# Attention times values on TensorE's two halves, in a kernel of windowed attention and a gated spatial mixer

## The chip, the cores and the metric

The kernel runs on one core of a Trainium2 chip. A core has five engines that run side by side and meet through semaphores: TensorE (PE, matrix products into PSUM), VectorE (DVE), ScalarE (ACT), GpSimd (POOL) and SyncE (SP), which here issues all DMAs. PSUM has eight banks of 512 float32 words for each of 128 partitions. The metric is the device time in microseconds (us) from one launch, inputs and output in HBM; lower is better.

## What is computed

One transformer layer for 2048 tokens of width 448, in bfloat16: normalisation, attention of 16 heads of 28 over 8 keys at distances 0, 2, ..., 14 back, a residual; then normalisation and a gated mixer whose gate is a 2048 x 2048 product over tokens.

```python
qkv = (x @ wqkv).reshape(B, S, 3, H, Dh)            # H=16, Dh=28, x normalised
idx = pos[:, None] - 2 * arange(8)[None, :]         # keys of a query; mask idx >= 0
logits = einsum('bhsd,bhswd->bhsw', q, kg) * Dh ** -0.5
attn = softmax(where(mask, logits, -1e9))
o = einsum('bhsw,bhswd->bhsd', attn, vg)            # attention times values
h = x + o.reshape(B, S, D) @ wo

z = gelu(layernorm(h) @ w_in)                       # 2 x 896 columns
z1, z2 = z[..., :896], layernorm(z[..., 896:])
g = einsum('ts,bsf->btf', w_sp, z2) + b_sp[None, :, None]
out = h + (z1 * g) @ w_out
```

## The kernel before

The attention works on 18 blocks of queries (112 to 128 tokens, GEOM, L17), each with 128 keys. The logits of a block are computed dense, keys by queries, head by head (L763, keys on the partitions); ACT takes exp of them into E (L772), and DVE multiplies E by a band mask that leaves the eight distances (L778, called mk below). Values carry a 29th column of ones (V1), so that one product gives both the weighted sum and the softmax's denominator: for each of 16 heads a matmul with E as the 128 x 128 stationary operand and 29 moving columns of V1 (L783 to L791, jobs o0 to o17). All 16 go into one PSUM bank, 32 words for a head. DVE takes the reciprocal of the 29th column (L795) and multiplies the other 28 by it (L798) into otm. A DMA transpose brings otm into OT (oT0 to oT17), for the later blocks by way of OTs and a copy (oc), and the projection with wo follows for pairs of 128 tokens (project, L720: y0, y2, ...), then the residual sum, the second normalisation and its transposes hT into hnT.

Most other products contract 448 = 7 x 64 rows, so they run in halves of the array: product (L486) pairs a matmul on rows 0 to 63 with one on rows 64 to 127, for two outputs in two banks. Its job A has four pairs and its job B three; in B the two halves of the array change banks, so that B waits for A's last matmul (`pl.apart`, own). Some other PE job must stand between A and B; the planner asserts it. Such products are qk (queries and keys), v, y, z1 and z2 (the two halves of the mixer's input). The logits use quarters of the array (28 rows). Full-array work is that of the values, the first transposes xT0 to xT3 (L647), the spatial product (L908) and the output product (L932). The code calls the three modes F (full), H (half) and L (quarter); SWITCH (L20) holds the planner's own costs for going from one to another.

Nothing is ordered at run time: every piece is a job with an engine; ORDER lists the jobs' numbers, and each engine runs its jobs in that sequence. BANK gives each product's first PSUM bank, ON says for some copies whether ACT, DVE or POOL makes them. Number 912 in ORDER is a filler matmul that keeps PE busy at the start. SP runs DMAs in its own sequence: tokens, weights, the transposes xT4 to xT15 of the normalised tokens, the oT and hT transposes, w_in, and 32 transposing loads of the spatial weights (wsp_la, wsp_lb, wsp_hi). Before a query/key product of 512 tokens can start, its four xT must have landed.

Of the kernel before, what the change touches and what calls it, by code (L numbers as in the profile page):

```python
# [6 lines left out]
D = 448  # L7
NHEAD = 16
DH = 28
# [16 lines left out]
ORDER = [21, 36, 112, 24, 22, 25, 0, 37, 38, 1, 44, 45, 35, 39, 40, 46, 47, 2, 116, 3, 121, 23, 912, 912, 912, 912, 912, 912,  # L26
# [82 lines left out]
ALU = mybir.AluOpType  # L109
# [213 lines left out]
def bass_sequential_preLN__sliding_local_dilated__mixer_gmlp__prompt_kernel(  # L323
# [12 lines left out]
    pl = Planner()  # L336
# [4 lines left out]
    with contextlib.ExitStack() as top:  # L341
# [404 lines left out]
        for b in range(NAB):  # L746
# [33 lines left out]
            tk = Ticket(1)  # L780
            vs = b % NV

            def fo(e, nq=nq, slot=slot, vs=vs, tk=tk):  # L783
                for g in range(4):
                    for hh in range(4):
                        h, ei = 4 * g + hh, 4 * hh + g
# [221 lines left out]
```

## Time and profile before

| | us |
|---|---|
| three runs | 240.85, 243.95, 241.71 (median 241.71) |
| the profiled execution | 240.89 |
| its span, first to last instruction | 239.2 |

The span is what the profile's rows lie in; 1.7 us of the execution lie around it. In the profile, a group's row gives line, engine, operation, output and inputs, shapes and count, then busy us, mean ns of one, and the engine's idle time just before, with what ended it. A row of the timeline gives start, length from the first start to the last end, engine, line and count; a bracket at its end is the idle time before it. The matmuls overlap one another, so their mean duration is longer than the interval at which they start.

### The profile page before, as it was taken

The numbers are of one execution on the slowest core, as the hardware profiler recorded it, in microseconds if no ns is written. First come the engines' busy times: TensorE is split into PE (matmuls) and PEld (weight loads), VectorE is DVE, ScalarE is ACT, GpSimd is POOL, SyncE is SP. The second block draws the span as 40 slices with busy tenths as digits, with TensorE's granted clock in tenths as the row PEclk, the third lists the DMA queues.
The fourth block names the chain that finished last, engine by engine and source line by source line (L and its number), as shares of the span: only waits on it lengthen the run. The fifth ranks groups of instructions, "written<-read, shape, count | busy, mean of one in ns | idle before, by whom it ended". The sixth has DMA issues, their size and how long they took to land.

```text
span 239.2 us, 4969 instructions
## 1 busy us (share of the span) xinstructions
PE 231.4 (97%) x2099; PEld 114.3 (48%) x2110; DVE 152.3 (64%) x323; ACT 92.0 (38%) x113; POOL 35.2 (15%) x73
## 2 busy tenths in 40 slices
PE   7989999799999999999999999999999999999995
PEld 2564464354555644444444444444444444444453
DVE  5799799979989987959877124410751222613674
ACT  3787988768789656687820000000000000000000
POOL 5154220440302030313124000000000000000000
DMA  6943538526668967979999970000000010000032
GB/s 202 340 119 69 137 70 142 89 60 124 148 106 165 171 108 157 154 149 165 168 192 166 186 189 0 3 0 0 0 0 3 31 47 0 0 3 0 26 108 97
DMA packets 66310, 23.26 MB, mean 97 GB/s; under 512 B 58608, under 2 KB 66160, under 8 KB 66288
## 3 DMA queue, kind: packets, MB, share of 16 engines
q1 hardware_dynamic: 66288, 22.95, 47.1%
q8 instruction: 16, 0.26, 0.4%
q14 instruction: 6, 0.05, 0.1%
HBM read 6.83 MB, written 1.84 MB: 36 GB/s over the span
## 4 chain that ended last, share of the span: by engine, by line
PE 81%; DVE 9%; DMA 4%; ACT 2%; SPq 2%; issue 1%; POOL 0%
PE psum L908 40%; PE psum L495 27%; PE psum L932 9%; DMA x_tm<-in_A_x_dram 3%; PE psum L763 2%; PE psum L787 2%; DVE st L607 2%; DVE E L778 2%; DMA xhT<-xn 2%; ACT E L772 1%; DVE z2p L505 1%; DVE otm L798 1%; SPq L520 1%; SPq L519 1%; DVE xn L618 1%
## 5 line engine op out<-in xcount | busy, mean ns | idle before, releaser
L908 PE MATMUL psum<-wsp_hi,z2p 128*128 128x512 bf16 x218 | 50.6, 379 | 0.3
L917 DVE TENSOR_TENSOR ub<-psum,bb 128x512 bf16<-128x512 f32 x28 | 19.2, 689 | 44.4 <-PE psum L908 43.9
L772 ACT ACTIVATE E<-psum 128x896 bf16<-128x896 f32 (+2 forms) x36 | 32.0, 934 | 9.0 <-PE psum L763 9.0
L908 PEld LDWEIGHTS psum<-wsp_hi,z2p 128*128 128x128 bf16 x224 | 21.9, 98 | 26.1
L495 PE MATMUL psum<-xhT,wqk 64*128 64x512 bf16 (+1 forms) x280 | 27.1, 334 | 2.0 <-DMA xhT<-xn 1.6
L908 PE MATMUL psum<-wsp_lb,z2p 128*128 128x512 bf16 x108 | 26.1, 379 | 0.2
L908 PE MATMUL psum<-wsp_la,z2p 128*128 128x512 bf16 x111 | 25.9, 379 | 0.2 <-issue 0.2
L495 PE MATMUL psum<-w_in,hnT 64*128 64x448 bf16 x224 | 24.8, 349 | 0.1
L495 PE MATMUL psum<-hnT,w_in 64*128 64x512 bf16 x196 | 24.1, 376 | 0.0
L939 DVE TENSOR_TENSOR srg<-psum,x_tm 128x448 bf16<-128x448 f32 (+1 forms) x17 | 9.7, 592 | 20.8 <-PE psum L932 20.7
L932 PE MATMUL psum<-w_out,z1p 128*128 128x448 bf16 (+1 forms) x119 | 22.3, 341 | 0.0
L843 DVE BATCH_NORM_STATS2 st<-z2p 128x6 f32<-128x448 bf16 x32 | 18.9, 609 | 3.7 <-ACT z2p L836 3.4
L778 DVE TENSOR_TENSOR E<-E,maskb 128x1792 bf16<-128x1792 bf16 (+2 forms) x18 | 19.6, 1095 | 1.7 <-ACT E L772 1.6
L607 DVE BATCH_NORM_STATS2 st<-x_tm 128x6 f32<-128x448 bf16 x32 | 19.4, 612 | 1.6 <-DMA x_tm<-in_A_x_dram 1.4
L602 POOL TENSOR_TENSOR rs<-rs,negh 128x2 f32<-128x2 f32 (+2 forms) x22 | 18.9, 857 | 1.8
L495 PEld LDWEIGHTS psum<-xhT,wqk 64*128 64x128 bf16 x280 | 12.8, 94 | 12.3 <-ACT E L772 2.4
L908 PEld LDWEIGHTS psum<-wsp_la,z2p 128*128 128x128 bf16 x112 | 10.9, 98 | 13.4 <-DVE z2p L852 0.4
L908 PEld LDWEIGHTS psum<-wsp_lb,z2p 128*128 128x128 bf16 x112 | 11.0, 98 | 13.2
L932 PEld LDWEIGHTS psum<-w_out,z1p 128*128 128x128 bf16 x119 | 11.6, 98 | 10.2 <-DVE z1p L920 0.3
L880 ACT ACTIVATE z1p<-psum 128x1024 bf16<-128x1024 f32 x14 | 14.2, 1023 | 5.2 <-PE psum L495 5.1
L495 PEld LDWEIGHTS psum<-w_in,hnT 64*128 64x128 bf16 x224 | 10.6, 94 | 11.0 <-DVE z2p L505 0.6
L601 POOL TENSOR_SCALAR rs<-mv 128x2 f32<-128x2 f32 (+2 forms) x22 | 6.3, 288 | 62.1 <-DVE mv L609 41.3
(54 smaller groups left out, 226.2 us busy)
## 6 DMA issues: line engine op xcount, KB each, us to landing
w_in<-in_B_w_in_dram SPq DMA_DIRECT2D x8, 224.0 KB, 3.0
out_dram<-srg SPq DMA_DIRECT2D x16, 112.0 KB, 1.7
x_tm<-in_A_x_dram SPq DMA_DIRECT2D x3, 448.0 KB, 6.1
wraw<-in_A_wqkv_dram SPq DMA_DIRECT2D x2, 448.0 KB, 4.1
w_out<-in_B_w_out_dram SPq DMA_DIRECT2D x1, 784.0 KB, 6.4
bb<-in_B_b_sp_dram SPq DMA_DIRECT2D x1, 512.0 KB, 5.8
wv<-in_A_wqkv_dram SPq DMA_DIRECT2D x2, 224.0 KB, 6.3
wo<-in_A_wo_dram SPq DMA_DIRECT2D x1, 336.0 KB, 7.7
```

Of the source, the lines that this page charges most:

```text
L495: ins = e.matmul(out(k), w(k, p0, c), x(k, p0, c), start=(k, p0, c) in first, stop=(k, p0, c) in last, tile_position=(p0, 0))
L601: [(lambda e: e.tensor_single_scalar(A, mv[:, m:m + n, 1], EPS, ALU.add), r_mv[k][m:m + n], [rr]), (lambda e: e.tensor_tensor(R, A, negh[: ...
L602: (lambda e: e.tensor_tensor(R, A, negh[:, 0:1].to_broadcast([128, n]), ALU.pow), [rr, r_negh], r_rs[k][m:m + n])],
L607: [(lambda e: e.bn_stats(st[:, m, :], src), [rsrc], [r_st[k][m]])], dve_t(D))
L772: return e.activation(o, i, AF.Exp, scale=SCALE)
L778: return e.tensor_tensor(a, a, maskb[:, 0:1, pad:pad + nq].to_broadcast([NK, NHEAD, nq]), ALU.mult)
L843: [(lambda e, m=m, k=k: e.bn_stats(st3[:, m, k, :], z2p[:, m, D * k:D * (k + 1)]), [r_z2[m]], [r_st[2][m]])], dve_t(D))
L880: return e.activation(o, i, AF.Gelu_apprx_tanh)
L908: ins = e.matmul(psv(tk), z2p[:, s, 128 * fc:128 * fc + 128], w[:, 512 * (tc % 2):512 * (tc % 2) + 512], start=(s == 0), stop=(s == NB - 1))
L917: [(lambda e, tc=tc, s=s, tk=tk: e.tensor_tensor(ub[:, s, :], psv(tk), bb[:, 512 * tc:512 * tc + 512], ALU.add), [r_bb], [r_ub[s]])], dve_ ...
L932: ins = e.matmul(psv(tk, 0, c1 - c0), z1p[:, fc, 128 * m:128 * m + 128], w_out[:, fc, c0:c1], start=(fc == 0), stop=(fc == FC7 - 1))
L939: [(lambda e, m=m, s=s, tk=tk, c0=c0, c1=c1: e.tensor_tensor(srg[:, s, c0:c1], psv(tk, 0, c1 - c0), x_tm[:, m, c0:c1], ALU.add), [r_x[m]], ...
```

## The change

The 16 matmuls of a block, each with all 128 keys, become 32, each with 64 keys: rows 0 to 63 of the array for the first half of the keys, rows 64 to 127 for the second. The block has two banks now, with eight heads in each. In job A the lower half of the array works on the eight heads of the first bank and the upper half on those of the second; in job B they change banks, so each head's sum is completed in PSUM by the second of its matmuls. Only the first matmul in each bank clears it (start), and the last closes it (stop). B waits for A as in product. DVE's two readers address two banks; they read as many elements as before.

With 18 jobs more, ORDER, BANK and ON are new as a whole: the order of all engines' work changes, and some copies change engine. Of the large casts, DVE has qe1_1, qe1_2, qe4_3, ve6 and four z2 casts before, and qe1_1, qe3_0, qe3_1 and two z2 casts after. The filler stands 16 times instead of 13.

```diff
-ORDER = [21, 36, 112, 24, 22, 25, 0, 37, 38, 1, 44, 45, 35, 39, 40, 46, 47, 2, 116, 3, 121, 23, 912, 912, 912, 912, 912, 912,
+ORDER = [21, 36, 0, 23, 26, 27, 112, 1, 22, 2, 116, 24, 3, 35, 37, 38, 44, 39, 45, 46, 47, 40, 117, 122, 120, 930, 930, 930,
...
-            tk = Ticket(1)
+            tk = Ticket(2)
...
-            def fo(e, nq=nq, slot=slot, vs=vs, tk=tk):
-                for g in range(4):
+            def fo(e, part, nq=nq, slot=slot, vs=vs, tk=tk):
+                for gg in range(2):
                     for hh in range(4):
-                        h, ei = 4 * g + hh, 4 * hh + g
-                        ins = e.matmul(psum[:, tk.b * 512 + 32 * h:tk.b * 512 + 32 * h + DH + 1],
-                                       E[:, slot, ei * nq:ei * nq + 128], V1[:, vs, h, 0:DH + 1],
-                                       start=True, stop=True)
+                        for r in range(2):
+                            k = part ^ r
+                            ei = 4 * hh + 2 * k + gg
+                            c = (tk.b + k) * 512 + 32 * (4 * gg + hh)
+                            ins = e.matmul(psum[:, c:c + DH + 1], E[64 * r:64 * r + 64, slot, ei * nq:ei * nq + 128],
+                                           V1[64 * r:64 * r + 64, vs, 4 * (2 * k + gg) + hh, 0:DH + 1], start=part + gg + hh == 0, stop=part + gg + hh == 5,
+                                           tile_position=(64 * r, 0))
                 return ins
-            o_jobs[b] = pl.job("o%d" % b, "pe", b + KEY["o"], [(fo, [r_E[slot], r_V[vs]] + r_Eh[slot], [])], 0.40, acq=tk)
+            ro = [r_E[slot], r_V[vs]] + r_Eh[slot]
+            oa = pl.job("o%dA" % b, "pe", b + KEY["o"], [(lambda e, fo=fo: fo(e, 0), ro, [])], 0.25, acq=tk, kind="H")
+            o_jobs[b] = pl.job("o%dB" % b, "pe", b + KEY["o"], [(lambda e, fo=fo: fo(e, 1), ro, [])], 0.25, acq=tk, kind="H")
+            pl.apart.append((oa, o_jobs[b]))
+
+            def pso(tk, nq):
+                return psum[0:nq, tk.b * 512:tk.b * 512 + 1024].rearrange("p (k x) -> p k x", k=2)[:, :, 0:256].rearrange("p k (h d) -> p k h d", d=32)
...
-                return e.reciprocal(rcp[0:nq, rsl, :], psv(tk, 0, 512, nq).rearrange("p (h d) -> p h d", d=32)[:, :, DH])
+                return e.reciprocal(rcp[0:nq, rsl, :].rearrange("p (k h) -> p k h", k=2), pso(tk, nq)[:, :, :, DH])
```

Three places show the new order. In these rows V_81 is V1, E the masked weights, xhT the transposed tokens, and lines of the changed kernel are one higher up to L780 and ten higher after it at DVE's readers (L805 and L808 for L795 and L798).

First, PE at the first values. Before, the two first blocks' values and those of the third stand between query/key products (L495) and logits (L763):

```order
L495 MATMUL psum<-xhT,wqk 128x512 x40
L787 MATMUL psum<-V_81,E 128x29 x32
L763 MATMUL psum<-qkT 128x112 x8
L495 MATMUL psum<-xhT,wqk 128x512 x8
L763 MATMUL psum<-qkT 128x112 x16
L787 MATMUL psum<-V_81,E 128x29 x16
L495 MATMUL psum<-xhT,wqk 128x512 x6
```

The same place after:

```order
L764 MATMUL psum<-qkT 128x112 x16
L496 MATMUL psum<-wv,xhT 128x448 x6
L496 MATMUL psum<-xhT,wqk 128x512 x22
L791 MATMUL psum<-V_81,E 128x29 x16
L496 MATMUL psum<-xhT,wqk 128x512 x6
L791 MATMUL psum<-V_81,E 128x29 x16
L496 MATMUL psum<-xhT,wqk 128x512 x8
L791 MATMUL psum<-V_81,E 128x29 x16
L496 MATMUL psum<-xhT,wqk 128x512 x6
L791 MATMUL psum<-V_81,E 128x29 x32
```

A block's values now come as two pieces of 16, each between pieces of half-array products, and no longer beside the logits; single pieces of values are what separates the 8 (job A) from the 6 (job B) of a product.

Second, SP around the transposes of the tokens. Before, eight xhT transposes stand together, two of w_in follow, and the last four (tokens 1536 to 2047) are spread among the first five of OT:

```order
L519 DMA_TRANSPOSE xhT<-xn 128x4x128 x8
L520 DMA w_in<-in_B_w_in_dram 128x896 x2
L519 DMA_TRANSPOSE OT<-otm 128x4x128
L519 DMA_TRANSPOSE OT<-otm 128x4x112 x2
L520 DMA w_in<-in_B_w_in_dram 128x896 x2
L519 DMA_TRANSPOSE xhT<-xn 128x4x128
L519 DMA_TRANSPOSE OT<-otm 128x4x112 x2
L519 DMA_TRANSPOSE xhT<-xn 128x4x128 x3
```

After:

```order
L520 DMA_TRANSPOSE wsp_la<-in_B_w_sp_dram 128x1024
L520 DMA_TRANSPOSE xhT<-xn 128x4x128 x5
L520 DMA_TRANSPOSE wsp_la<-in_B_w_sp_dram 128x1024
L520 DMA_TRANSPOSE xhT<-xn 128x4x128 x3
L521 DMA w_in<-in_B_w_in_dram 128x896
L520 DMA_TRANSPOSE OT<-otm 128x4x128
L520 DMA_TRANSPOSE OT<-otm 128x4x112
L520 DMA_TRANSPOSE xhT<-xn 128x4x128
L521 DMA w_in<-in_B_w_in_dram 128x896
L520 DMA_TRANSPOSE xhT<-xn 128x4x128
L520 DMA_TRANSPOSE OT<-otm 128x4x112
L520 DMA_TRANSPOSE xhT<-xn 128x4x128 x2
```

Two loads of spatial weights have come in among the first eight, and the last four now stand among the first three of OT. On PE the first product of the last tokens moves ahead of one query/key product of the tokens before them (qk3_3), of v8 and y2, of five logits and of the values of two blocks.

Third, DVE ahead of the copies from OTs that the projection y10 (tokens 1280 to 1535) needs. Before, a mask, two normalisations and a cast stand around the first copy, and the projection comes later on PE:

```order
L731 TENSOR_TENSOR x_tm<-psum,x_tm 128x896
L607 BN_STATS st_63<-x_tm 128x6
L778 TENSOR_TENSOR E<-E,maskb 128x1824 x2
L505 CAST z2p<-psum 128x896
L609 BN_AGGR mv_64<-st_63 128x2
L778 TENSOR_TENSOR E<-E,maskb 128x1824
L609 BN_AGGR mv_64<-st_63 128x2
L843 BN_STATS st_65<-z2p 128x6
L778 TENSOR_TENSOR E<-E,maskb 128x1824
L618 TENSOR_SCALAR xn<-x_tm,mv_64,rs_68 128x512
L505 COPY OT<-OTs 128x4x114
```

After:

```order
L732 TENSOR_TENSOR x_tm<-psum,x_tm 128x896
L608 BN_STATS st_63<-x_tm 128x6
L619 TENSOR_SCALAR xn<-x_tm,mv_64,rs_68 128x512 x4
L779 TENSOR_TENSOR E<-E,maskb 128x1824
L506 COPY OT<-OTs 128x4x114 x2
L779 TENSOR_TENSOR E<-E,maskb 128x1824
L608 BN_STATS st_63<-x_tm 128x6
L779 TENSOR_TENSOR E<-E,maskb 128x1824
L732 TENSOR_TENSOR x_tm<-psum,x_tm 128x896
```

Two copies now stand together behind the residual sum of y8 (the first row), a statistic, four normalisations and one mask.

More of the change, by code (lines that the diff above doesn't have):

```diff
@@ L75 @@
 WINB = 2
-ON = {'xe0_0': 'act', 'xe0_1': 'act', 'xe1_0': 'act', 'xe2_0': 'act', 'xe3_0': 'dve', 'wp0_0_0': 'act', 'wp0_1_0': 'act',
[4 rows of a table removed]
-    'act', 'qe4_3': 'dve', 've0': 'act', 'od0': 'dve', 'od1': 'pool', 've2': 'act', 'od2': 'pool', 'od3': 'pool',
-    've4': 'act', 'od4': 'dve', 'od5': 'pool', 've6': 'dve', 'od6': 'dve', 'od7': 'pool', 've8': 'act', 'od8': 'dve',
-    'od9': 'dve', 've10': 'act', 'od10': 'pool', 'od11': 'pool', 'oc11': 'dve', 've12': 'act', 'od12': 'pool', 'oc12':
-    'dve', 'od13': 'dve', 'oc13': 'act', 've14': 'act', 'od14': 'dve', 'oc14': 'dve', 'od15': 'dve', 'oc15': 'act',
-    've16': 'act', 'od16': 'pool', 'oc16': 'dve', 'od17': 'pool', 'oc17': 'dve', 'z2c1': 'act', 'z2c2': 'dve', 'z2c3':
-    'dve', 'z2c4': 'act', 'z2c5': 'act', 'z2c6': 'dve', 'z2c7': 'dve', 'z2c8': 'act', 'z2c9': 'act', 'z2c10': 'act',
+ON = {'xe0_0': 'act', 'xe0_1': 'act', 'xe1_0': 'act', 'xe2_0': 'dve', 'xe3_0': 'act', 'wp0_0_0': 'dve', 'wp0_1_0': 'dve',
[5 rows of a table added]
+    'act', 'od4': 'pool', 'od5': 'pool', 've6': 'act', 'od6': 'dve', 'od7': 'pool', 've8': 'act', 'od8': 'pool',
+    'od9': 'pool', 've10': 'act', 'od10': 'dve', 'od11': 'pool', 'oc11': 'act', 've12': 'act', 'od12': 'dve', 'oc12':
+    'dve', 'od13': 'dve', 'oc13': 'dve', 've14': 'act', 'od14': 'pool', 'oc14': 'dve', 'od15': 'dve', 'oc15': 'dve',
+    've16': 'act', 'od16': 'pool', 'oc16': 'dve', 'od17': 'pool', 'oc17': 'dve', 'z2c1': 'act', 'z2c2': 'act', 'z2c3':
+    'act', 'z2c4': 'act', 'z2c5': 'dve', 'z2c6': 'act', 'z2c7': 'act', 'z2c8': 'act', 'z2c9': 'act', 'z2c10': 'dve',
     'z2c13': 'act'}
@@ L792, in bass_sequential_preLN__sliding_local_dilated__mixer_gmlp__prompt_kernel @@
             rsl, os = b % 4, b % NO
             def fr(e, nq=nq, rsl=rsl, tk=tk):
-                return e.reciprocal(rcp[0:nq, rsl, :], psv(tk, 0, 512, nq).rearrange("p (h d) -> p h d", d=32)[:, :, DH])
+                return e.reciprocal(rcp[0:nq, rsl, :].rearrange("p (k h) -> p k h", k=2), pso(tk, nq)[:, :, :, DH])
             def fmul(e, nq=nq, rsl=rsl, os=os, tk=tk):
-                return e.tensor_tensor(otm[0:nq, os, 0:D].rearrange("p (h d) -> p h d", d=DH),
-                                       psv(tk, 0, 512, nq).rearrange("p (h d) -> p h d", d=32)[:, :, 0:DH],
-                                       rcp[0:nq, rsl, :].unsqueeze(2).to_broadcast([nq, NHEAD, DH]), ALU.mult)
+                return e.tensor_tensor(otm[0:nq, os, 0:D].rearrange("p (k h d) -> p k h d", k=2, d=DH), pso(tk, nq)[:, :, :, 0:DH],
+                                       rcp[0:nq, rsl, :].rearrange("p (k h) -> p k h", k=2).unsqueeze(3).to_broadcast([nq, 2, 8, DH]), ALU.mult)
```

2 lines of the change are left out of this document (1 added, 1 removed), and 96 rows, old and new, of tables (BANK, ON, ORDER).

## The prediction

> **What bounds the kernel now.** I read the page's busy line first, then busy time by stage, then the matmul groups, then the rows where TensorE (PE) stood still.
>
> ```profile
> PE 231.4 (97%) x2099; PEld 114.3 (48%) x2110; DVE 152.3 (64%) x323; ACT 92.0 (38%) x113; POOL 35.2 (15%) x73
> 0.00:7.60 7.60, 5.76 (x21) 2.03 (x21) 4.26 (x12) 3.65 (x8) 3.44 (x14) 1.00 0.72 217
> 7.60:118.60 111.00, 108.28 (x1522) 57.04 (x1524) 98.00 (x213) 85.66 (x104) 27.57 (x51) 1.00 0.71 137
> 118.60:236.60 118.00, 117.32 (x556) 55.24 (x565) 49.70 (x100) 2.73 (x4) 4.23 (x8) 1.00 0.24 52
> 236.60:239.20 2.60, 0.00 (x0) 0.00 (x0) 0.37 (x1) 0.00 (x0) 0.00 (x0) 1.00 0.35 113
> ```
>
> The stage rows give, after the length, the busy time of PE, PE's weight loads, DVE, ACT and POOL. There are four stages: a start without real matmuls (7.6 us), attention with the first products (111.0), the 2048 x 2048 spatial product with the output product (118.0), and a tail (2.6). PE fills the two long ones at clock 1.00. The change's new matmuls lie in the second stage alone, and there DVE is busy for 98.0 of 111.0 us, so it is almost a second bound: work that PE saves is worth something only where DVE and the transposing DMAs deliver.
>
> ```profile
> L787 PE MATMUL psum<-V,E 128*128 128x29 bf16 x288 | 9.0, 176 | 0.0
> L763 PE MATMUL psum<-qkT 28*128 28x112 bf16 x144 | 4.7, 210 | 0.0
> L495 PE MATMUL psum<-xhT,wqk 64*128 64x512 bf16 x168 | 20.3, 377 | 1.6 <-DMA xhT<-xn 1.6
> 12.74 0.72 PE L647 MATMUL psum<-ident,xn 128*128 128x128 bf16 x8 [0.80 <-DVE xn L618]
> 47.41 1.04 PE L495 MATMUL psum<-xhT,wqk 64*128 64x512 bf16 x8 [1.62 <-DMA xhT<-xn]
> ```
>
> The last two rows are PE's only long waits in that stage: 0.80 us for the normalised tokens 256 to 511 and 1.62 us for the transposed last tokens. In all PE waits 111.0 - 108.3 = 2.7 us there. That sets a floor: without any of it and without the 1.3 us of mode changes worked out below, the profiled execution would take 240.9 - 2.7 - 1.3 = 236.9 us, so a gain over 2% needs all of it, or cheaper matmuls.
>
> The profiled execution took 240.89 us, with a span of 239.2. My sum is against 240.89; the median of the three runs shown, 241.71, is 0.8 above it.
>
> **The change, part by part.**
>
> ```profile
> 27.03 0.81 PE L495 MATMUL psum<-xhT,wqk 64*128 64x512 bf16 x6
> 27.77 0.96 PE L787 MATMUL psum<-V,E 128*128 128x29 bf16 x32
> 28.67 0.37 PE L763 MATMUL psum<-qkT 28*128 28x112 bf16 x8
> 28.97 1.04 PE L495 MATMUL psum<-xhT,wqk 64*128 64x512 bf16 x8
> 15.90 0.40 PE L763 MATMUL psum<-qkT 28*128 28x128 bf16 x16
> ```
>
> *Mode changes.* A row's length runs to the end of its last matmul, so its last start is start + length - one duration. The six half-array matmuls (pairs side by side, as all of L495): last start 27.03 + 0.81 - 0.38 = 27.46; eight of them (28.97, 1.04) make four pairs, so a pair takes (1.04 - 0.38)/3 = 0.22; the array is free at 27.68 and the full-array values start at 27.77: 0.09 us lost. Values to quarter-array logits: last start 27.77 + 0.96 - 0.18 = 28.55, free 0.03 later, next start 28.67: again 0.09. Logits to halves: last start 28.67 + 0.37 - 0.21 = 28.83, free 0.05 later, next start 28.97: 0.09. Counted through PE's order, from the first query/key product to the spatial product, the mode changes 55 times before and 40 times after, since the values no longer leave the half mode. 15 x 0.09 = **-1.3 us**; all this is on PE, the path. The three prices hardly differ: -1.2 to -1.5.
>
> *The multiplications.* Before: 288 with 128 rows, one each (0.96 - 0.18)/31 = 25 ns, in all 7.2 us. After: 576 with 64 rows, in pairs on the two halves. No row has so short a matmul in half mode. The lower end is by columns: 512 take 0.22 us a pair, so 29 take 12 ns, 288 x 12 = 3.5 us, 3.7 less. The upper end is 25 ns for each, one after another: 14.4 us, 7.2 more. The nearest row is the last above: 16 quarter-array matmuls, each with its own weights, (0.40 - 0.21)/15 = 13 ns apart, so four strips do not queue behind one another for 25 ns. I take 25 ns a pair, each half behaving as the whole array does now: **0 us**. The Trainium skill, "TensorE: Matmul & The Clock Gate", Part 1 ("Wait — 56ns, not 53.3ns?"), says that starts are never closer than about 25 ns however few the columns. The trace agrees on one strip and disagrees on four; by that rule the sum would be 7.2 us higher.
>
> *The second half's wait.* Both halves of a block write the same two banks, so the second waits until the first has ended. In about 15 places only 16 small matmuls, 0.20 us, stand between the two halves of a product (of values or of a projection). A 512-column matmul lasts 0.38 by its group and its successor may start 0.22 after it; 0.22 + 0.20 = 0.42 against 0.38 plus the handing over, which I bound by 0 and 0.1 (the mode change, the dearest handover seen on PE). So 0 to 1.5 us; I take half a handover each, **+0.7 us**.
>
> *DVE's readers.* Reciprocal and multiplication read the same 16 and 448 elements, now from two banks:
>
> ```profile
> L798 DVE TENSOR_TENSOR otm<-psum,rcp 112x448 bf16<-112x448 f32 x9 | 5.6, 624 | 0.3
> L795 DVE RECIPROCAL rcp<-psum 112x16 f32<-112x16 f32 x9 | 2.2, 250 | 1.1 <-PE psum L787 1.1
> L505 DVE CAST z2p<-psum 128x896 bf16<-128x896 f32 x4 | 4.3, 1084 | 2.0 <-PE psum L495 2.0
> L505 DVE CAST qkT<-psum 128x1024 bf16<-128x1024 f32 x1 | 1.2, 1225 | 0.0
> L505 DVE CAST V<-psum 128x896 bf16<-128x896 f32 x1 | 1.1, 1092 | 0.0
> L505 ACT ACTIVATE wqk<-wraw 128x224 bf16<-128x224 bf16 x2 | 0.7, 394 | 0.0
> ```
>
> The element count decides these durations (16 take 250 ns, 448 take 624), so **0 us**, ends -0.2 and +1 (18 x 0.05). In the table of engines DVE loses two of four z2 casts (2 x 1.08) and one of V (1.09), and has two 1024-column query/key casts for one (+1.2): about 2 us less in a stage where it has 13 us free. ACT takes them on. That is worth nothing by itself; it goes into the waits below.
>
> *The start.* PE's first product waits for the unpacked weights and two transposed tiles. After, ACT has a weight copy between the second and the first tile's copies and the second tile is normalised first; I add **+0.2 us** (half a weight copy, 0.39), ends 0 and 0.4. In return v0's second half stands before the transposes that waited 0.80.
>
> *The new order's waits*, by three places:
>
> ```profile
> 14.39 5.24 SPq L519 DMA_TRANSPOSE xhT<-xn  x4
> 37.93 0.40 DVE L618 TENSOR_SCALAR xn<-x_tm,mv,rs 128x512 bf16<-128x512 bf16 x1
> 40.56 4.97 SPq L519 DMA_TRANSPOSE xhT<-xn  x3
> xhT<-xn SPq DMA_TRANSPOSE x12, 2.5
> L778 DVE TENSOR_TENSOR E<-E,maskb 128x1792 bf16<-128x1792 bf16 x9 | 9.8, 1086 | 1.7 <-ACT E L772 1.6
> ```
>
> (1) SP issues a transpose every 1.3 us (5.24/4), which lands 2.5 us after its start (median). The four for tokens 512 to 1023 cannot be out earlier than before, and PE, ahead by the filled 0.80, asks for them earlier: 0.5 to 1.0 us. (2) Before, the last of the four tiles of the last tokens was normalised at 37.93, but three of their transposes were issued from 40.56 until 45.53 only, and PE, which wanted them at 47.41 - 1.62 = 45.8, had to wait. After, the last normalisation has the same six masks ahead of it on DVE, two reciprocals and multiplications and a V cast fewer (2 x 0.87 + 1.09), two query/key casts more (2 x 1.2): it ends at 38.3 - 2.8 + 2.4 = 37.9, and SP has only its transpose left: landed at 40.4. PE wants it earlier too, by three products of 14 matmuls (7 pairs of 0.22 at most, 4.6), five logits (0.2 each) and two values (0.4 each): 45.8 - 6.4 = 39.4. So 1.0 us, ends 0 and 2. (3) The projection of tokens 1280 to 1535 (y10) needs a copy of OTs on DVE that now stands behind a residual sum, a statistic, four normalisations and a mask: 0 to 1.4 us, where PE had no wait. Together 0.5 to 4.4 against 2.7 now; I take the middle, 2.5: **-0.2 us**, ends -2.2 and +1.7. A cover that goes: every block's values now hold two banks, so two banks at a time, four pairs in all, are all there is, and what is late next is ACT's reading of the logits.
>
> In the third stage the same matmuls stand in another order; PE had no wait there and gets none in my sum, since the wsp_la and wsp_lb transposes are issued no later than before.
>
> Sum: -1.3 + 0 + 0.7 + 0 + 0.2 - 0.2 = -0.6 us, so 240.89 - 0.6 = **240.3 us**.
>
> **Rivals.**
> *A. 25 ns for each matmul.* Against it: 13 ns apart on four strips. For it: no row shows two strips with less than 112 columns, and eight logits lie (0.37 - 0.21)/7 = 23 ns apart. It gives 240.3 + 7.2 = 247.5, slower. It decides from about 23 ns each on (10.8 ns above 12.5, x 576 = 6.2 us, which is 246.5). Chance 0.10. The Trainium skill's page "TensorEngine Tiling (Array Packing)", "Instruction Overhead", points the same way: a matmul with one column takes as long as one with 60, so small ones gain nothing by tiling.
> *B. DVE or the transposes hold PE.* All three places at their upper end, and the second half's waits too: 240.9 - 1.3 + 1.5 + 0.2 + 1.7 = 243.0; with one more late transpose (2.5) 245.5. For it: DVE 98.0 of 111.0. Chance 0.20, nearly all within 2%.
> *C. Cheap pairs and a full PE.* 12 ns a pair and few waits: 240.9 - 1.3 - 3.7 + 0.2 - 1.0 = 235.1. Against it: one strip never went under 25 ns. Chance 0.08.
> *D. The change does not reach the path*: the mode changes saved are waited off elsewhere: 240.9. Chance 0.17, indistinguishable from the forecast.
>
> **How the numbers follow.** The forecast has 0.45. Its own range is 238 to 243, the ends of its terms not all falling together. A (0.10) lies above, and the better half of C below, so 237.0 to 244.5 leaves out about 0.17. Two per cent, about what a measurement of this kernel can tell from no change, is 4.8 us of 241.71: faster below 236.9, slower above 246.5. Faster: C, 0.08. Slower: A, and 0.03 of B, 0.13. Within: 0.79.
>
> **What would show it.** Right: 16 small matmuls in a row about 0.38 us long by the timeline (0.20 and one duration of 0.18), no 0.09 us gap beside them, first spatial matmul at 117 to 119 us. Wrong by A: 0.55 us for 16. Wrong by B: DVE or xhT<-xn as releaser of PE waits over 2 us. Wrong by C: 16 in 0.28 us. The forecast as a whole is wrong if the third stage is no longer 118 us.

## The result, and the profile after

The changed kernel takes 244.86 us (median of 19 runs, 243.47 to 248.89), the kernel before 242.11 (median of 19, 240.68 to 244.26): a ratio of 1.0121, 95% interval 1.0094 to 1.0147. Three of the 19 runs, of 247.4 to 248.9 us, lie over 1.5% above the fastest and are not in that ratio. The changed kernel is 1.2% slower: less than the 2% that separate "faster" and "slower" here, but a difference that the interval tells from none, and above the range of the forecast. The profiled execution of the changed kernel took 244.86 us too, with a span of 243.1. It is 4.0 us longer than the profiled execution before, the medians lie 2.75 apart: that one was among the shortest of its kernel, so the rows below show the loss about 1.2 us too large.

The page's busy line of the changed kernel:

```profile
PE 232.6 (96%) x2401; PEld 117.4 (48%) x2401; DVE 150.7 (62%) x323; ACT 94.0 (39%) x113; POOL 30.2 (12%) x73
```

Its busy time by stage, columns as before (length; then PE, its weight loads, DVE, ACT, POOL):

```profile
0.00:8.10 8.10, 6.12 (x24) 2.29 (x24) 4.66 (x15) 3.62 (x8) 4.95 (x20) 1.00 0.75 233
8.10:122.40 114.30, 108.41 (x1811) 59.79 (x1810) 99.74 (x219) 88.01 (x104) 22.30 (x47) 1.00 0.69 131
122.40:240.40 118.00, 118.00 (x569) 55.35 (x567) 45.86 (x90) 2.35 (x3) 2.93 (x6) 1.00 0.25 53
```

The third stage is 118.0 us as before, the clock 1.00 throughout. The start is 0.5 us longer (8.1 for 7.6), the second stage 3.3 (114.3 for 111.0). There PE is busy as long as before (108.4 for 108.3) and stands still for 114.3 - 108.4 = 5.9 us where it stood still for 2.7. The loss is in waits. PE's, by releaser (total us, times, longest; the 1.5 us of L956 lie in the start; left out are 0.5 us of L648, in the start too, and 0.2 us for a DMA):

```profile
PE psum L496 <- ACT V L506: 2.9, 1, 2.9
PE psum L956 <- DVE warm L577: 1.5, 1, 1.5
PE psum L496 <- DVE otm L808: 0.8, 1, 0.8
PE psum L496 <- ACT xhT L506: 0.7, 1, 0.7
PE psum L764 <- DVE otm L808: 0.6, 1, 0.6
PE psum L764 <- DVE qkT L506: 0.5, 1, 0.5
```

Three of these places, and values beside the first, in the timeline (start, length, group, idle before it):

```profile
24.03 2.55 PE L496 MATMUL psum<-xhT,wqk 64*128 64x512 bf16 x22 [2.91 <-ACT V L506]
26.41 0.37 PE L791 MATMUL psum<-V,E 64*128 64x29 bf16 x16
26.61 0.82 PE L496 MATMUL psum<-xhT,wqk 64*128 64x512 bf16 x6
...
66.64 0.37 PE L764 MATMUL psum<-qkT 28*128 28x114 bf16 x8 [0.57 <-DVE otm L808]
...
71.70 0.93 PE L496 MATMUL psum<-wo,OT 64*128 64x448 bf16 x8 [0.76 <-DVE otm L808]
```

At 24.03 starts the first query/key product of tokens 512 to 1023 (qk2). The row names ACT's copy of V as releaser, but that copy was done at 23.26. The last of the four transposes that the product reads, xT5, landed at 23.83 by its semaphore, 0.2 us before the product starts: the releaser is that DMA. The values behind it are what the forecast said: 16 small matmuls in 0.37 us.

### The profile page after: what moved, and what is told of

It is laid out like the page before. It is cut to its first block, busy times and chain, and to the rows that moved or that the text cites. A ratio compares the mean times of both kernels' runs of the same rounds, so it can differ in the third digit from the quotient of the medians.

```text
span 243.1 us, 5565 instructions
## 1 busy us (share of the span) xinstructions
PE 232.6 (96%) x2401; PEld 117.4 (48%) x2401; DVE 150.7 (62%) x323; ACT 94.0 (39%) x113; POOL 30.2 (12%) x73
## 3 DMA queue, kind: packets, MB, share of 16 engines
q1 hardware_dynamic: 66288, 22.95, 46.4%
## 4 chain that ended last, share of the span: by engine, by line
PE 77%; DVE 11%; ACT 5%; DMA 2%; POOL 2%; issue 1%; POOLq 0%
PE psum L917 40%; PE psum L496 24%; PE psum L941 9%; ACT E L773 3%; DVE st L852 2%; DVE st L608 2%; DVE x_tm L732 2%; PE psum L791 2%; PE psum L764 2%; DMA hnT<-xn 2%; DVE E L779 1%; POOL rs L603 1%; DVE otm L808 1%; DVE xn L619 1%; DMA x_tm<-in_A_x_dram 1%
## 5 line engine op out<-in xcount | busy, mean ns | idle before, releaser
L773 ACT ACTIVATE E<-psum 128x896 bf16<-128x896 f32 (+2 forms) x36 | 31.4, 931 | 4.1 <-PE psum L764 3.9
L496 PE MATMUL psum<-xhT,wqk 64*128 64x512 bf16 (+1 forms) x280 | 28.3, 334 | 3.7 <-ACT V L506 2.9
L852 DVE BATCH_NORM_STATS2 st<-z2p 128x6 f32<-128x448 bf16 x32 | 18.3, 610 | 1.0 <-ACT z2p L845 1.0
L506 ACT ACTIVATE qkT<-psum 128x1024 bf16<-128x1024 f32 (+1 forms) x17 | 14.3, 855 | 8.7 <-PE psum L496 8.7
L603 POOL TENSOR_TENSOR rs<-rs,negh 128x2 f32<-128x2 f32 (+2 forms) x22 | 16.8, 762 | 1.8
```

The costliest lines, as they stand in the source:

```text
L496: ins = e.matmul(out(k), w(k, p0, c), x(k, p0, c), start=(k, p0, c) in first, stop=(k, p0, c) in last, tile_position=(p0, 0))
L506: j = pl.job(name, eng, key, [(lambda e: e.activation(o(), i(), AF.Copy) if eng == "act" else e.tensor_copy(o(), i()), list(reads), list(w ...
L603: (lambda e: e.tensor_tensor(R, A, negh[:, 0:1].to_broadcast([128, n]), ALU.pow), [rr, r_negh], r_rs[k][m:m + n])],
L773: return e.activation(o, i, AF.Exp, scale=SCALE)
L852: [(lambda e, m=m, k=k: e.bn_stats(st3[:, m, k, :], z2p[:, m, D * k:D * (k + 1)]), [r_z2[m]], [r_st[2][m]])], dve_t(D))
```

## Experiments

Each ratio is that to the kernel before, from runs on the same chip at the same time. "Landing" is the last of a DMA's 16 semaphore updates. Where only ORDER is edited, the diff gives the jobs' names in the order of their engine.

**1. wlo2 out of the way.** The new order puts a load of spatial weights on SP ahead of the four transposes.

```diff
 x12
-wlo2
 xT7
...
 oT0
+wlo2
 oT1
```

> The changed kernel with one row moved: wlo2, a transposing load of spatial weights, stands on SP behind oT0 instead of ahead of the transposes of tokens 512 to 1023. Theory 1 (wlo2 in front of them makes the last of the four land late, at 23.83 us): the last one lands about 1 us or more earlier, at 22.8 or before, the query/key product of tokens 512 to 1023, which stood still for 3.07 us, waits under 1.5 us, and the time falls by 1.5 to 3 us, to 242 to 243.5. Rival (engine work on a shared DMA engine, above all the fetches of PE's instructions at 20.05 and 20.88, holds the last transpose, wherever wlo2 stands): the last one still lands after 23 us, the wait stays over 2 us, and the time falls by less than 1 us. Second rival (the wait is ACT's copy of V, which the profile names as releaser): the wait stays 3 us and does not follow the landing.

244.14 us, ratio 1.0097 (1.0069 to 1.0125): against 1.0121, no gain that the intervals tell apart. The rows are from an execution of 248.52 us, whose granted clock fell only at 69 us, behind what is read here. The wait did shrink: xT5 landed at 22.38, qk2 started at 22.58, 0.2 us behind it as before, after an idle time of 1.1 us; so the second rival is out. PE was 1.46 us earlier than in the changed kernel, until 40.26, where y0 waited 1.3 us for oT2, which had landed at 40.13, and the last tokens' product started later than in the changed kernel (43.01 for 42.79). The first half of theory 1 holds, the gain in time does not: SP's next transposes landed hardly earlier than in the changed kernel (oT2 at 40.13 for 40.40) or later (the last tokens' xT13 at 42.81 for 42.36). The first rival is half right: xT5 still landed 2.8 us after the end of its issue (3.6 in the changed kernel), with a fetch of PE's instructions at 20.35.

**2. The converse in the kernel before.**

```diff
 x12
+wlo2
 xT5
```

> The kernel before with one row moved: wlo2 stands on SP ahead of the transposes of the first tokens 512 to 1023, where the changed kernel has it. Theory 1 (that place is what makes them late): the last of the four, which landed at 20.84 us, lands 1 us or more later, the query/key product behind it, which started at 21.20 without a wait, waits 0.5 to 3 us, and the time rises by 0.5 to 3 us. Rival (fetches of instructions in the changed kernel do it, and wlo2 is harmless): landings move by less than 0.7 us, the wait is under 0.3 us, the time is the same within 0.5 us.

241.86 us, ratio 0.9995 (0.9956 to 1.0034). The four landed 0.8 to 0.9 us later (17.69 to 21.74, before 16.89 to 20.84), and qk2 waited:

```profile
21.88 1.47 PE L495 MATMUL psum<-xhT,wqk 64*128 64x512 bf16 x12 [0.41 <-DMA xhT<-xn]
```

So wlo2 costs 0.9 us of landing and half a microsecond of waiting, not 3, and nothing in time. It is not the cause by itself. Nor does it hold SP: its own issue was over at 12.27, and the first of the four was issued at 14.49, when its tile was normalised (14.39 before). But that issue took 2.06 us for 1.30, beside a fetch of PE's instructions at 15.04, which came at 13.73 before. In the four profiled executions with wlo2 in front this fetch comes at 14.45 to 15.04, in the eleven others at 13.13 to 14.03; why is not shown.

**3. The halved values in the old order.**

```diff
-ORDER, BANK, ON of the changed kernel
+ORDER, BANK, ON of the kernel before, each oN as oNA and oNB; o0, o6, o13 in another pair of banks;
+o3, o10, o16, o17 behind the readers of the pairs that they need
+on PE v12B and z2_5B, on DVE some rows moved with them
```

> The halved attention-times-values, but in the order of rows of the kernel before and with its choice of engines; a few value products stand up to four rows later, because each now holds two banks. Mode changes in stage two: 46, against 55 before and 40 in the changed kernel. Theory (the halving itself costs nothing, the new order's waits cost the time): the first spatial product starts at 118 to 120 us, the time is that of the kernel before within 1 us either way (-0.8 for nine mode changes fewer, +0.7 for the second halves' waits, some tenths for rows that wait for a pair of banks). Rival (the halved form itself costs, by its two banks at a time or by its small matmuls): 2 to 4 us slower than before, as the changed kernel is.

264.11 us, ratio 1.0878 (1.0808 to 1.0948): both theories missed by some 20 us. PE's waits, with their releasers (total us, times, longest):

```profile
PE psum L764 <- DVE otm L808: 3.4, 4, 1.6
PE psum L496 <- DMA hnT<-xn: 2.6, 1, 2.6
PE psum L764 <- DVE qkT L506: 2.1, 1, 2.1
PE psum L496 <- DVE otm L808: 1.8, 2, 1.0
PE psum L791 <- DVE otm L808: 1.8, 2, 1.0
```

And the stage as a whole (the clock is the third number from the end):

```profile
8.00:140.00 132.00, 115.42 (x1774) 59.65 (x1776) 95.62 (x207) 82.86 (x100) 25.85 (x51) 0.91 0.55 108
```

Logits, products and values wait for DVE's multiplication by the reciprocal, which reads a block's banks: two of the four pairs where two blocks stand together, as the old order has them. PE stood still for 132.0 - 115.4 = 16.6 us, and the clock was 0.91 on the mean there, which is 0.09 x 132 = 12 us more. The second bank has a price, and the old order cannot pay it; a new order was part of the change. (My placing of the rows is one of many, so 264 is no bound.)

**4. The new order with values on the whole array.**

```diff
-                for gg in range(2):
+                for g in range(2):
                     for hh in range(4):
-                        for r in range(2):
-                            k = part ^ r
...
+                        gg = 2 * part + g
+                        ei = 4 * hh + gg
+                        c = (tk.b + part) * 512 + 32 * (4 * g + hh)
+                        ins = e.matmul(psum[:, c:c + DH + 1], E[:, slot, ei * nq:ei * nq + 128],
+                                       V1[:, vs, 4 * gg + hh, 0:DH + 1], start=True, stop=True)
```

> The changed kernel's order, but the sixteen multiplications of a block stay on the whole array (128 rows), eight heads in each of two banks, each bank's eight in a job of its own. Mode changes in stage two: 92 against 40. By the price of the forecast (0.09 us each) that is 52 x 0.09 = 4.7 us more, less 0.6 us for second halves that need no longer wait for the first: 4.1 us slower than the changed kernel, about 249. Rival (a mode change costs what a matmul's end costs anyway, and the halving saves nothing): within 1 us of the changed kernel. A spatial product that starts at 126 to 127 us would show the first, at 122 to 123.5 the second.

248.95 us, ratio 1.0287 (1.0222 to 1.0353), 4.1 us above the changed kernel. Values and their neighbours:

```profile
25.90 0.36 PE L790 MATMUL psum<-V,E 128*128 128x29 bf16 x8
26.20 0.82 PE L496 MATMUL psum<-xhT,wqk 64*128 64x512 bf16 x6
26.95 0.36 PE L790 MATMUL psum<-V,E 128*128 128x29 bf16 x8
```

The second stage:

```profile
8.60:126.20 117.60, 113.01 (x1523) 57.65 (x1525) 100.11 (x219) 88.67 (x104) 22.39 (x47) 1.00 0.64 127
```

Eight on the whole array take as long as 16 on halves. The stage is 3.3 us longer than in the changed kernel although PE stands still 1.3 us less (4.6 for 5.9): 4.6 us more of other time for 52 mode changes more, 0.09 us each. A mode change costs what the forecast took, and in this order the halving saves some 4 us: what made the changed kernel slower is its order, not its matmuls.

**5. 128 waits on a long-reached value, behind the fillers.**

```diff
             fn(eng).then_inc(sems[prod], inc)
+            if exe == "pe" and pad > 0:
+                pad -= 8
+                for _ in range(8):
+                    eng.wait_ge(sems["dve"], 1)
```

> The changed kernel with 128 waits added on PE, eight behind each of the first sixteen filler matmuls, on a semaphore value long reached: no work moves, but PE's instruction stream is 128 longer, half of the 256 between two of its fetches (16,384 bytes each, at 14.80, 20.05, 31.15, 37.47 and 43.58 us in the changed kernel). Theory (a fetch makes the transposes beside it land about 2 us late and one issue about 1 us longer): the fetches lie at about 16.5, 27.5 and 33 us, and with them the long issues of SP and the late landings; the last transpose of tokens 512 to 1023, which took 3.6 us from the end of its issue to its landing, takes under 2 us unless a fetch of another engine falls there, the wait of 3.07 us falls under 2 us. Rival (the late landing belongs to that transpose or to its place behind wlo2): it lands 3 us or more after its issue, and the wait stays above 2.5 us.

248.82 us (one run). The fetch that came at 20.05 came at 20.60, still beside xT5, which landed at 23.87, 3.3 us after the end of its issue; the waits had delayed PE by 1.3 us at 9 us. The fetch did not move by enough: nothing told.

**6. SP cleared, first placing.** Six loads go from SP's rows of 9 to 46 us to where SP was idle for 6 us.

```diff
-wlo2, wlo6, w_in1_0, w_in0_1, w_in0_0, wlo4   (among xT7 to xT13 and oT0 to oT5)
...
 oT8
+w_in1_0, w_in0_1, w_in0_0, wlo2, wlo6, wlo4
 oT9
```

> The changed kernel with six rows of SP moved: the loads of spatial weights wlo2, wlo6 and wlo4 and of w_in1_0, w_in0_1 and w_in0_0, in all 3 x 1.30 + 3 x 0.58 = 5.6 us of issuing, stand behind oT8, where SP was idle for 6.0 us, instead of among the transposes of 9 to 46 us; all other engines keep their rows. Theory (SP, which issues one transpose per 1.27 us and loses about 1 us more to an issue beside a fetch of PE's instructions, holds PE at tokens 512 to 1023 and, as the run with wlo2 moved alone showed, again at y0 and at the last tokens): the waits at these three places fall from 3.6 us to under 1.5 us in all, qk4_3 starts at 41 us or before (42.8 in the changed kernel), and the time falls by 1.5 to 2.5 us, to 242 to 243. Rival (behind SP stands DVE, busy without a break from 55 to 73 us, and takes whatever PE gains before): qk4_3 starts earlier too, but waits of logits and y8 at 65 to 76 us grow by as much, and the time falls by less than 0.7 us.

247.36 us, ratio 1.0210 (1.0154 to 1.0265): slower. Yet the waits that experiment 1 had met at y0 and at the last tokens were gone, and PE was 1.27 us ahead until 66.9 us. Then the waits between 64 and 72 us:

```profile
PE psum L764 <- DVE otm L808: 3.2, 2, 2.6
DVE otm L808 <- DMA OT<-otm: 2.9, 1, 2.9
```

And the stretches there:

```profile
67.00:69.00 2.00, 0.00 (x0) 0.00 (x0) 0.18 (x1) 0.89 (x1) 0.00 (x0) 1.00 0.88 157
69.00:76.00 7.00, 6.50 (x76) 3.15 (x76) 5.06 (x11) 3.17 (x4) 0.00 (x0) 0.51 0.52 116
```

oT9, issued at 64.77 behind the moved loads (64.38 in the changed kernel) and with a fetch at 66.31 beside its landing, landed at 68.73 (66.73 in the changed kernel); DVE waited for the buffer that it reads, PE for the banks that DVE reads; and when PE went on, its granted clock was 0.51 for 7 us, 3.4 us lost. The moved loads are not needed for this: in experiment 1, with nothing moved there, oT9 was issued at 64.53, a fetch came at 66.97, it landed at 69.04, PE waited 1.5 us and the clock fell.

**7. The same with two normalisations forward.**

```diff
 n0_15
+n0_14
+n0_13
 qe3_1
-n0_14
...
-n0_13
```

> The run with SP's six rows moved, and on DVE besides the normalisations n0_14 and n0_13 of the last tokens ahead of two casts of queries and keys and two masks (2 x 1.22 + 2 x 1.08 = 4.6 us). Theory that the last normalisation holds qk4_3 once SP is free: its last transpose is issued before 38 us, no wait at qk4_3, another 0.5 to 1 us faster than with SP's rows alone. Rival (the casts and masks that are now late hold PE as much): the wait appears at the products and logits of 34 to 42 us instead, the time is the same or longer.

248.37 us, ratio 1.0252 (1.0198 to 1.0306). The last transpose, xT13, landed at 40.72 for 40.96; but experiment 6 had no wait left there, so there was nothing to gain. The wait at 70 us stayed (2.3 us).

**8. SP cleared, second placing.**

```diff
 oT8
+w_in1_0, w_in0_1, w_in0_0
 oT9
...
 hT6
+wlo2, wlo6, wlo4
 whi0
```

> As in the run with six rows of SP moved, but only w_in1_0, w_in0_1 and w_in0_0 (0.43 to 0.58 us each) stand behind oT8; wlo2, wlo6 and wlo4 stand behind hT6, far behind oT9. In that run the waits at y0 and at the last tokens were gone and PE was 1.27 us ahead of the changed kernel until 66 us; there oT9, issued at 64.77 behind the moved loads and beside a fetch at 66.31, landed at 68.73 instead of 66.73, om12 on DVE waited 2.9 us for its buffer, lg15_1 on PE 2.7 us for the bank that om12 reads, and the granted clock fell to 0.50 from 69 to 76 us. Theory (that wait is my six rows' doing and the transposes' place on SP is what counts all along): oT9 is issued at 63.1 to 63.3 and lands before 66 us, no wait over 1 us at lg15_1, clock 1.00, and the time is 242 to 243.5, 1 to 2 us below the changed kernel. Rival (whatever is gained before 60 us is lost behind it, on DVE or to the clock): a wait of 1 us or more stands between 60 and 80 us, and the time is within 0.7 us of the changed kernel or above it.

247.64 us, ratio 1.0190 (1.0136 to 1.0245). oT9 landed at 65.47, PE had no wait there and led by 1.5 us until 90 us. Then oT14, now behind three more loads and beside two fetches, held y12:

```profile
93.17 0.94 PE L496 MATMUL psum<-wo,OT 64*128 64x448 bf16 x8 [2.78 <-DVE OT L506]
```

```profile
93.00:96.00 3.00, 2.83 (x20) 1.30 (x22) 1.75 (x5) 0.73 (x1) 0.24 (x1) 0.66 0.53 107
```

The rival holds: a wait moved on, and the clock fell again.

**9. v4 into the wait at 22 to 24 us.**

```diff
 lg2_1
-lg2_0
 v2B
+v4A
+lg2_0
+v4B
 qk2_1A
```

> The run before this one with one row of PE moved besides: v4, the values of tokens 512 to 639, which needs only the first of the four transposes of tokens 512 to 1023, stands ahead of their query/key products, with a logit between its halves and its two halves' 1.65 us in the wait there; its copy on ACT moves with it, and three products change their banks. Theory (PE waits there for the last of the four transposes, at 22.4 to 23.8 us, and for nothing else): v4 fills the wait, qk2_1 starts at the landing with less than 0.3 us of PE idle, PE is 1.2 to 1.7 us earlier than without it from 36 us on, and some of that, 0.3 to 1 us, is lost again at the last tokens, whose transposes are no earlier; in all 0.5 to 1.3 us faster than the run before. Rival (PE is held by DVE behind): the same time.

249.01 us, ratio 1.0282 (1.0221 to 1.0343). A mistake of mine: v4 covers tokens 512 to 767 and reads xT5 as well, the last to land (22.50), so v4 itself waited until 22.64. The run tells nothing of the theory.

**10. SP cleared, third placing.**

```diff
 oT4
+wlo2, wlo6
 wlo4
 oT5
...
 oT8
+w_in1_0, w_in0_1, w_in0_0
 oT9
```

Behind oT4 is where the changed kernel has wlo4 already, so five loads move.

> As in the two runs with six rows of SP moved, in a third placing: w_in1_0, w_in0_1 and w_in0_0 behind oT8, wlo2, wlo6 and wlo4 (3 x 1.30 us) behind oT4, where SP was idle for 4.8 us in the first of the two. In the second PE was 1.3 to 1.5 us ahead of the changed kernel until 92 us, and only there lost 2.9 us to y12, whose transpose oT14 stood behind the three loads that had been put at 77 to 81 us, and more to the clock. Theory (SP's rows are the price, wherever they stand ahead of a block's transposes): with no load left ahead of a transpose that PE waits for, the lead of 1.3 to 1.5 us holds to the spatial product, which starts at 120.7 to 121.5 us at clock 1.00, and the time is 242 to 243.5. Rival (each placing meets another late transpose, since a fetch comes every 5 to 8 us and SP has too little slack anywhere): again a wait over 1 us at some other place, and no gain over the changed kernel.

243.80 us, ratio 1.0059 (1.0029 to 1.0089), an interval below that of the changed kernel. The lead of 1.05 us held to 69 us; 0.4 of it went at y8, whose banks DVE had yet to read; the timeline there, then the stage:

```profile
71.07 0.93 PE L496 MATMUL psum<-wo,OT 64*128 64x448 bf16 x8 [1.18 <-DVE otm L808]
```

```profile
8.60:121.60 113.00, 108.35 (x1811) 59.83 (x1810) 99.50 (x218) 87.99 (x104) 22.32 (x47) 1.00 0.70 130
```

The same matmuls with 4.7 us of waits for 5.9; the start, 0.5 us later in this execution (8.59), took some of it back. By the ratios SP's rows are worth about 0.6%, half of the loss. But it is not shown that the waits are that half: the mean granted clock was under 0.999 in one of the 12 executions here and in 8 of 19 of the changed kernel, and the medians of the others, 243.73 and 243.90 us, hardly differ. Most of the gain lies in how often the clock fell, and in the runs of the kernel before beside them (242.65 here, 242.11 there).

**11. v4 forward, with xT4 and xT5 first.** As 10, with v4 as in 9, and besides:

```diff
-xT7, xT4, xT6, xT5
+xT5, xT4, xT6, xT7
```

> The run before this one with the values v4 ahead of the query/key products of tokens 512 to 1023, as tried before, but with what v4 reads mended: it reads the transposes xT4 and xT5, and xT5 was the last of the four, so in that try v4 itself waited until 22.64 us. Here xT5 and xT7 have changed places on SP, and their normalisations on DVE, so that xT4 and xT5 land by about 18.2 us. Theory (the wait at 22 to 24 us is for the last transpose alone): v4's 1.65 us of PE work runs from about 21 us on, qk2_1 follows at the last landing, 22.5 us, or when v4 and one logit are done, about 22.8, and PE is 1.3 to 1.7 us ahead of the run before this one at 36 us; some 0.5 to 1 us is lost again at the last tokens' transposes; the time is 0.5 to 1.3 us below that run, about 241.5 to 242.5. Rival (DVE or ACT hold PE behind): the same time within 0.4 us.

244.37 us, ratio 1.0072 (1.0040 to 1.0104). The wait at 22 to 24 us was gone altogether, but of its 1.7 us nothing arrived: o0, at 26.70, then waited for a pair of banks (1.37 us after the array could have taken it), in the row of the waits:

```profile
PE psum L791 <- ACT qkT L506: 1.2, 1, 1.2
```

**12. Other banks for o0 and o2.** As 11, with BANK alone changed.

```diff
-o0: banks 2, 3; o2: banks 4, 5
+o0: banks 4, 5; o2: banks 2, 3
```

> The run with v4 ahead, with two pairs of banks changed: o0 in the pair that v4's copy on ACT frees at 24.4 us, o2 in the pair of the first query/key product. In that run the wait for the last transpose at 22 to 24 us was gone, but o0 waited 1.37 us at 26.70 for a pair of banks that I had given it and that ACT's copy of a query/key product freed only at 26.55. Theory (that pair of banks took the gain): o0 starts by 25.5 us without a wait over 0.3 us, PE is 1.0 to 1.4 us earlier from there on, some of it lost at the last tokens, and the time is 242.5 to 243.5, below both runs. Rival (ACT or the last tokens' transposes hold PE behind): a wait of about 1 us moves to 30 to 43 us and the time stays at 243.5 to 244.5.

244.35 us, ratio 1.0075 (1.0048 to 1.0102). o0 did not wait; qk2_3, whose banks o2 now had, waited instead:

```profile
29.64 1.04 PE L496 MATMUL psum<-xhT,wqk 64*128 64x512 bf16 x8 [0.82 <-DVE otm L808]
```

The wait moved to the next user of the banks, a little ahead of where the rival put it. No version tried beats the kernel before.

**13. A fetch moved.** As 10, with waits on a long-reached value ahead of two jobs on PE.

```diff
+            if exe == "pe" and fn is not None and k in (32, 42):
+                for _ in range(60 if k == 32 else 46):
+                    eng.wait_ge(sems["dve"], 1)
```

> The third placing of SP's rows with 106 waits more on PE, on a value long reached: 60 ahead of the query/key product at 14.7 us, where PE waits 0.84 us, and 46 ahead of the logits at 19.2 us, where it waits 0.65 us, some 10 ns each, so that no work moves; only the fetch of PE's instructions that came at about 20.3 us should come 1 to 2 us earlier. Theory (a transpose beside a fetch lands late, whichever it is): with the fetch at 18.3 to 19.3 us it is xT6, whose issue ended at 18.46 and which landed 1.2 us later, that now lands 2.5 us or more after its issue, and the issue of xT5 behind it takes about 2 us instead of 1.27. Rival (it belongs to xT5, to its place or to its data): xT6 lands 1.2 us after its issue, xT5 3 us after, as before. If the fetch does not move by 0.8 us, nothing is told.

249.45 us (one run). Not as planned: a wait cost about 0.03 us, not 0.01, so PE was held 2.2 and 1.3 us and the fetch came later, at 25.42, not earlier. But SP did at 14 to 20 us what it had done without the waits (xT5 issued at 18.45 to 19.72, in experiment 10 at 18.51 to 19.78), now with no fetch beside it: xT5 landed at 20.95, in experiment 10 at 22.95. DMA from 18 to 24 us in experiment 10 and here:

```profile
q8 instruction: 1, 0.02, 0.9%
q14 instruction: 1, 0.01, 0.7%
...
xhT<-xn SPq DMA_TRANSPOSE x4, 3.0
```

```profile
q14 instruction: 1, 0.01, 0.6%
...
xhT<-xn SPq DMA_TRANSPOSE x3, 2.5
```

Queue 8 brings PE's instructions, 16,384 bytes at a time. The same transpose in the same place, 2.0 us sooner without that packet; and xT9, which now had the fetch beside it, landed 2.8 us after the end of its issue. What also differs is that xT9 stands 3.8 us behind xT5 here and 0.3 behind it in experiment 10; but xT7, xT4 and xT6 each have the next one right behind them in both runs and land 1.2 us after their issue. So the late landing goes with the fetch, as far as one pair of executions can show it; a count over all of them is in the last section.

## Why the prediction was wrong

*The mode changes* (-1.3) were right, and together with *the second half's wait* (+0.7) they came out as forecast. The timeline counts idle time from the end of the last matmul; counted from when the array could have taken the next one, a wait costs the stream some 0.16 us more (0.38 less 0.22), and there are nine waits over 0.2 us so counted where there were four: 3.2 + 5 x 0.16 = 4.0 us. The stage is 3.3 longer, so the rest became 0.7 shorter, forecast 0.6. Experiment 4 gives the price of a change by itself: 0.09 us. The second half's wait alone was put too high: where 16 small matmuls separate two halves, the second starts 0.23 us after the first of them, and 0.20 where something else follows, so 0.03 us in each of 14 places, 0.4 in all. The forecast's own numbers (0.42 against 0.38 plus at most 0.1) allow 0.06 each, 0.9 in all and not 1.5.

*The multiplications* (0) were right, and rival A is refuted: the next product starts 0.20 us after 16 small matmuls began, 12.5 ns for each. So a pair on two halves takes the 25 ns that one matmul took on the whole array. The rule quoted from the Trainium skill, "TensorE: Matmul & The Clock Gate", Part 1, holds for each half by itself; the trace disagrees with it for the array as a whole.

*DVE's readers* (0) were right (624 and 252 ns for 624 and 250):

```profile
L808 DVE TENSOR_TENSOR otm<-psum,rcp 112x448 bf16<-112x448 f32 x9 | 5.6, 624 | 0.3
L805 DVE RECIPROCAL rcp<-psum 112x16 f32<-112x16 f32 x9 | 2.3, 252 | 1.8 <-PE psum L791 1.6
```

For DVE as a whole the forecast was off: its busy time fell by 1.6 us in all, but in the second stage, where about 2 less had been reckoned, it rose from 98.0 to 99.7.

*The start* (+0.2, at most 0.4) took 0.47, and 0.5 to 0.9 in the other profiled executions with the new order and nothing added at the start: a size.

*The new order's waits* (-0.2, at most +1.7) is the step that failed: +3.2 by the idle time, +4.0 by the stream. By its three places: (1) qk2 waited 2.91, forecast 0.5 to 1.0. The argument there was that SP issues a transpose every 1.3 us and it lands 2.5 us after its start; these are the usual values without a fetch beside it, and here one fetch (14.80) lengthened the issue of the first of four to 2.24 us and another (20.05) fell on the landing of the last. Of the 3.0 us by which the last landed later than before (23.83 for 20.84), 0.6 are its issue and 2.4 its landing. Before, the fetches came at 13.73 and 21.84, just ahead of the four and just behind them. (2) The last tokens' product waited 0.3 by the stream, forecast 1.0, but that was luck: the last normalisation ended at 39.33, forecast 37.9, its transpose landed at 42.36, forecast 40.4, and PE hardly waited because it was itself 3 us late. (3) y10 waited for nothing, forecast 0 to 1.4. And the three places were not all: the 0.80 us of the early transposes were filled, as forecast, but 0.7 and 0.5 us at 14.3 and 18.7, 0.57 at 66.64 and 0.76 at 71.70 had no term. The last two are for banks that DVE has yet to read. The prediction did name that cover ("two banks at a time, four pairs in all") and gave it no price.

The sum needed another reading too: places were priced one by one. Experiments 1, 6, 8, 11 and 12 each took a wait away, and each met the next one, 3 to 50 us further on. Rival B was the nearest (243.0, with one more late transpose 245.5), and by its own mark it is right: the releaser of the longest wait is xhT<-xn, with 2.91 us. It got 0.20; the forecast's own -0.2 had no wider ground than three rows. Of the forecast's own signs, the 16 small matmuls in 0.37 us, no gap beside them and a third stage of 118.0 us came true; the first spatial matmul did not, at 122.4 us for 117 to 119.

What stays open: which order would bring out the 0.7 us that the stream saves. By the ratios half of the loss went with SP's rows (experiment 10), though hardly by shorter waits; the rest I could only move about.

## What to carry to other kernels

Where a rearrangement takes more PSUM banks for each result, price it in the order that it forces: the multiplications came out exactly as forecast, and the time was lost in waits for banks and transposes. Take a DMA's time with its spread, not its median, wherever PE waits for the last of several; and when a wait is removed, follow the lead to the next late landing before counting it as a gain. The slack of a queue that seems idle off the path (SP here) is part of the price: of three placings of six loads, 5.6 us in all, one did no harm, and there one of the six was back in its old place.

## What the runs showed of the hardware

A fetch of PE's instructions slows the transposes beside it. Over all fifteen profiled executions, I took the 436 transposes xT and oT with either a queue 8 packet of 16,384 bytes starting between 1 us before their issue and 1 us after its end (173), or no fetch of any queue there (263): from the start of the issue to the landing the first took 3.72 us on the median (80% of them 2.70 to 4.39), the second 2.49 (2.41 to 2.71). In 65 of the 173 the issue on SP lengthens, from 1.27 to between 1.6 and 2.8 us; where the fetch starts after the issue has ended, it is the landing that is late. In 17 neither is seen. The 14 that had only a packet of queue 14 beside them took 2.53. It is a count, not a test: five of the six that took over 4 us with no fetch in that window stand right behind a load of w_in. The fetches follow PE's instruction count, one for about 256 of its records on the mean, so halves that double the matmuls bring more of them: 16 packets of that queue before, 19 after, 16 again in experiment 4.

PE's clock fell to half after waits of 2.6 us (experiment 6, 0.51 for 7 us) and 2.8 us (experiment 8), but also at 66.39 in experiment 12, where the only wait over 0.2 us in the 30 us before was one of 0.6 among logits; and it stayed at 1.00 after the 2.9 us at 24.03 in the changed kernel. Between the first product and the end of PE's work, every stretch at half clock in the fifteen profiled executions lasts 3.41 us or two or three times that, so that one of them costs at least 1.7 us, more than half of the loss in question. The Trainium skill, "TensorE: Matmul & The Clock Gate", Part 1, has the clock halve after an idle window of about 3.4 us that runs freely, and recover after a busy one. The half and the 3.41 us agree; the runs show the fall after far less than 3.4 us of waiting, and none after the 2.9 us. What decides it is open.
